# Attention times v in four 32-column tiles of the TensorE array instead of two 64-column tiles

## The chip, the cores and the metric

The kernel runs on one core of a Trainium2 chip. Its time is device microseconds (us) of one launch, as the median of several runs; the profile is one further execution, taken by the hardware profiler. PE is TensorE (matrix products and transposes), PEld its weight loads, DVE is VectorE, ACT is ScalarE, POOL is GpSimd, SP is SyncE, which issues most DMAs. L509 is line 509 of the kernel before; the change adds one line, so everything from L509 on has a number larger by one in the kernel after (L509 is L510 there, L519 is L520).

## The reference

The input is `q`, `k`, `v` of shape (4, 8, 768, 64): four batches, eight heads, 768 tokens, 64 numbers per head, all fp32. Two stages are computed.

```python
# attention: the first n_global = 8 keys, and the last n_local = 96 up to the query
scores = q @ k.T / sqrt(64) - slope[h] * dist          # masked outside the window
a      = softmax(scores)
x      = (a @ v)                                       # to (3072 tokens, 512)
# router and experts: one of 8 experts per token, by cosine similarity
logits = xn @ en.T / tau;  e = argmax(logits);  gate = softmax(logits)[e]
out    = gate * (relu(x @ w1[e]) @ w2[e])              # w1 512 x 1024, w2 1024 x 512
```

## The kernel before

**Two stages in time.** The window attention (`window_attention`) fills the time up to about 174 us of the profiled execution; the experts, at 512 to 576 slots each, take the rest. The change lies in the attention.

**How the attention is tiled.** A *group* is one batch with four heads (a half `m` of the eight); there are eight groups. The four heads are two *pairs* `a`, each with two heads `e`. A *unit* is a block `j` of 96 keys, eight per group, together with 30 copied rows of the global keys, which makes 126 rows (`ROWS`). A key block is seen by its own 96 queries and the next 96, so a unit has 192 columns of queries (the last one 96). A *step* works on two units of a group; there are 32 steps, and the order of work on PE, ACT, DVE and SP is written out by hand and kept (`manual_schedule` with these four engines). POOL is not among them in the attention: a planner places POOL's instructions, by times that it assumes for the others.

**What a step does.** `score` (L480) multiplies keys and queries into PSUM, in tiles of 64 rows by 32 columns of the array; `grow` (L486, ACT) takes the exponential into the tile `ex`; `weigh` (L493, DVE) multiplies it by a table of biases. Transposes on PE (L455, L550, L568, L582; full 128x128 array) turn k, q and the results of earlier groups. `attend` then works on the two units of the step before:

- products with v (L509): for each unit part and each pair `a`, one matmul for each of the two heads `e`. The weights are 126 rows by 64 columns of `v`, the moving operand is 192 or 96 columns of `ex`, and the output is 64 partitions of the PSUM tile `od[a]`;
- in every second step, the sums of the denominators (L519) for the parts of two steps: four matmuls per part, whose weights are 126 rows by 32 columns of the constant `halves`, and whose outputs lie side by side in four strips of 32 partitions of `od[2]`.

After the denominators, `od` is copied out (L524, L525, L530, L532). In some steps the experts' scores of an earlier half batch follow on PE (L559), also in weights of 32 columns (`enb`) with 128 rows, in four strips.

Each fp32 matmul appears in the trace as two weight loads and two MATMUL records: 288 matmuls of L509 are 576 records, and so are the 288 of L519.

**What else hangs on the change.** `load_v` loads each group's v by SP two groups ahead; its L430 on POOL copies the 30 global rows into all eight blocks, before the first L509 of that group. POOL also issues the scatters of the router's slots into DRAM (L257), each paced behind a step's score matmuls, and the square root of the router's norms (L224, `pow`), which DVE's L234 waits for.

Of the kernel before, what the change touches and what calls it, by code (L numbers as in the profile page):

```python
# [34 lines left out]
ROWS = BLK + GLB  # L35
# [341 lines left out]
def window_attention(k, ctx):  # L377
# [3 lines left out]
    nc, tc, NT, D, B, S, H, E = k.nc, k.tc, k.NT, k.D, k.B, k.S, k.H, k.E  # L381
# [113 lines left out]
    def attend(g, p, split=True):  # L495


        if p % 2 == 0:
            g.od = [po_p.tile([P, 512], F32, name="od%d" % i, tag="od%d" % i) for i in range(3)]
            k.free = g.od[2][:, QB * BLK :]  # L500
        parts = []
        if p == 2:
            parts.append((g.units[3], 0, BLK, 2 * BLK, True))
        for j in (2 * p, 2 * p + 1):
            parts.append((g.units[j], (j % QB) * BLK, 0, BLK if j % QB == QB - 1 else 2 * BLK, j == 0))
        for u, at, c0, c1, first in parts:
            for a in range(2):
                for e in range(2):
                    nc.tensor.matmul(g.od[a][e * D : (e + 1) * D, at : at + c1 - c0],  # L509
                                     lhsT=g.v[0:ROWS, 2 * a + e, u.j, :],  # L510
                                     rhs=u.ex[:, e, a, c0:c1], start=first, stop=True,
                                     skip_group_check=True)

        g.parts = parts = (g.parts if p % 2 else []) + parts
        for u, at, c0, c1, first in parts if p % 2 else []:
            for a in range(2):
                for e in range(2):
                    i = 2 * a + e
                    nc.tensor.matmul(g.od[2][32 * i : 32 * i + 32, at : at + c1 - c0], lhsT=k.halves[0:ROWS, g.m].rearrange("p i c -> p (i c)"),  # L519
                                     rhs=u.ex[:, e, a, c0:c1], start=first, stop=True,  # L520
                                     skip_group_check=True)
        if p % 2:
            xd = xd_p.tile([P, 2, QB * BLK], F32, name="xd", tag="xd")
            nc.scalar.copy(out=xd[:, 1, :], in_=g.od[1][:, 0 : QB * BLK])  # L524
            (nc.vector.tensor_copy if split else nc.scalar.copy)(out=xd[:, 0, :], in_=g.od[0][:, 0 : QB * BLK])  # L525
            g.xd.append(xd)
            h, den = p // 2, g.batch.den
            if g.m == 0:
                den[h] = den_p.tile([P, QB * BLK], F32, name="den", tag="den")
                nc.vector.tensor_copy(out=den[h][:], in_=g.od[2][:, 0 : QB * BLK])  # L530
            else:
                nc.vector.tensor_tensor(out=den[h][:], in0=g.od[2][:, 0 : QB * BLK], in1=den[h][:], op=ALU.add)  # L532
# [146 lines left out]
    for g in groups:  # L679
        g.units = []  # L680
        for j in range(NB):
            u = Net()
# [54 lines left out]
    for g in groups:  # L737
        gi = groups.index(g)
        pieces = [(g, a, i) for a in range(2) for i in (0, 2, 3, 1)]
        at = [4 * gi - 4 + i // 2 for i in range(8)]  # L740
        if gi == 0:
            pieces, at = [(g, a, i) for i in (3, 1) for a in range(2)], [0, 0, 1, 1]
        elif gi == 1:
            at = [2, 2, 2, 2, 3, 3, 3, 3]
        elif gi == 2:
            at = [5, 5, 5, 6, 6, 6, 7, 7]
        elif gi == len(groups) - 1:
            pieces = [(g, a, i) for i in (0, 2, 3, 1) for a in range(2)]
            at = [4 * gi - 4 + i for i in (0, 0, 0, 0, 1, 1, 2, 2)]
# [5 lines left out]
    for s, (g, p) in enumerate(steps):  # L755
# [60 lines left out]
        if s > 0:  # L816
            q, qp = steps[s - 1]
            attend(q, qp, s < len(steps) - 10)
            if q.m == 1 and qp % 2:
                waiting.append((prev, qp // 2))  # L820
# [15 lines left out]
    for hf in active:  # L836
        half_turns(hf)
        half_router(hf)
    attend(*steps[-1])
    scatter_later(k, len(k.later))  # L840
    hf = start_half(t, 1)
# [915 lines left out]
```

## Time and profile before

| | us |
|---|---|
| median of 3 runs (lowest, highest) | 528.84 (524.05, 530.36) |
| the profiled execution, its own time | 523.84 |
| its span, first to last instruction | 522.0 |
| busy PE / PEld / DVE / ACT / POOL | 498.9 / 411.8 / 301.8 / 197.5 / 152.5 |
| products with v, L509: PE busy, 576 records | 46.6 |
| sums of denominators, L519: PE busy, 576 records | 23.5 |

The first three rows are times of whole launches; the span leaves out 1.84 us around the instructions. Busy time of PE counts the time in which at least one matmul was under way, with its latency, so records that run side by side in different tiles of the array are counted once. The mean granted TensorE clock of the profiled execution is 0.997 of full speed.

### The profile page before, as it was taken

To read this page: it belongs to the slowest core of one execution; us is meant where nothing else is said; L and a number is where in the kernel's file an instruction comes from. 1 tells how busy PE (TensorE), PEld (TensorE's weight loads), DVE (VectorE), ACT (ScalarE), POOL (GpSimd) and SP (SyncE) were. 2 spreads that over 40 slices of the span, in tenths; PEclk is the share of its full clock that TensorE was granted. 3 is DMA by queue.
4 is the path that set the end of the run, shared out by engine and by line. 5 is a ranking of instruction groups with operands and counts; after the bars stand their busy time and mean duration, and the time that the engine had idled before them with its cause. 6 is when DMAs were issued, how large, how long until landed. Compare 5 with 4: busy or idle time off the path is not lost.

```text
span 522.0 us, 13699 instructions
## 1 busy us (share of the span) xinstructions
PE 498.9 (96%) x5606; PEld 411.8 (79%) x5606; DVE 301.8 (58%) x601; ACT 197.5 (38%) x494; POOL 152.5 (29%) x169
## 2 busy tenths in 40 slices
PE   8999999999988998999989999999999999999994
PEld 7777887876766687878878669989899689859963
DVE  5646777766786664938735616756656555615531
ACT  4966766767654321403212212322323222311210
POOL 4211121151364436353430034054043040022031
PEclk9999999999999999999999999999999999999998
DMA  9989988988632536767291028267075073001002
GB/s 171 198 186 174 225 227 209 219 189 201 153 103 79 151 58 151 240 209 265 85 331 44 2 68 317 106 211 249 4 240 218 4 247 139 2 25 58 0 22 68
DMA packets 111421, 76.32 MB, mean 146 GB/s; under 512 B 87077, under 2 KB 95269, under 8 KB 111281
## 3 DMA queue, kind: packets, MB, share of 16 engines
q1 hardware_dynamic: 102769, 59.00, 42.8%
q0 software_dynamic: 6912, 15.26, 9.0%
q8 instruction: 63, 1.03, 0.9%
q14 instruction: 77, 0.63, 0.5%
q10 hardware_dynamic: 1600, 0.39, 0.3%
HBM read 61.66 MB, written 17.16 MB: 151 GB/s over the span
## 4 chain that ended last, share of the span: by engine, by line
PE 56%; issue 2%; DVE 1%; DMA 1%; POOLq 0%; POOL 0%; DVEq 0%
PE big L1295 24%; PE big L1102 12%; PE work L1228 7%; PE work L1102 5%; PE work L1241 4%; PE work L1012 2%; PE big L1271 2%; DMA xg<-x_dram,idss 1%; PE work L1022 1%; POOL xg L986 0%; POOLq L1722 0%; DVE wsum L1041 0%; DVE y L1113 0%; DVE xsum L1042 0%; DVE xT L1041 0%
## 5 line engine op out<-in xcount | busy, mean ns | idle before, releaser
L493 DVE TENSOR_TENSOR ex<-ex,table 126x768 f32<-126x768 f32 x64 | 60.7, 955 | 41.8 <-ACT ex L486 41.2
L1307 DVE TENSOR_TENSOR hT<-big,hT 128x320 f32<-128x320 f32 (+4 forms) x70 | 39.3, 565 | 43.5 <-PE big L1295 42.1
L1247 POOL DMA_INDIRECT out_dram<-y_arm,tids x17 | 17.0, 1001 | 161.4 <-ACT y_arm L1230 120.1
L1295 PE MATMUL big<-xT,w1t 128*128 128x160 f32 (+4 forms) x336 | 59.4, 330 | 2.2 <-issue 2.2
L486 ACT ACTIVATE ex<-pa 126x384 f32<-126x384 f32 (+1 forms) x128 | 53.5, 476 | 21.1 <-PE pa L480 15.1
L1295 PEld LDWEIGHTS big<-xT,w1t 128*128 128x128 f32 x336 | 54.2, 190 | 4.9 <-issue 3.1
L986 POOL DMA_INDIRECT xg<-x_dram,idss x32 | 36.6, 1143 | 49.3 <-PE work L1012 15.9
L509 PE MATMUL od<-ex,v 126*64 126x192 f32 (+1 forms) x576 | 46.6, 305 | 0.2 <-issue 0.2
L480 PE MATMUL pa<-qT,kT 64*32 64x128 f32 (+3 forms) x2048 | 39.9, 268 | 2.5 <-issue 2.5
L480 PEld LDWEIGHTS pa<-qT,kT 64*32 64x32 f32 (+1 forms) x2048 | 30.1, 106 | 14.5 <-issue 10.9
L509 PEld LDWEIGHTS od<-ex,v 126*64 126x64 f32 x576 | 34.8, 136 | 8.2 <-issue 4.5
L1295 PE MATMUL big<-xsum,fsum 128*128 128x160 f32 (+4 forms) x224 | 39.7, 330 | 1.2 <-DVE hT L1307 1.2
L1015 ACT COPY xT<-work 128x256 f32<-128x256 f32 x56 | 18.0, 376 | 57.5 <-PE work L1012 54.0
L257 POOL DMA_INDIRECT meta<-mt,slot x24 | 27.7, 1153 | 39.7 <-DVE rd L553 20.0
L1295 PEld LDWEIGHTS big<-xsum,fsum 128*128 128x128 f32 x224 | 36.1, 190 | 2.6 <-DVE hT L1307 1.4
L1228 PE MATMUL work<-w2t,hT 128*128 128x512 f32 x80 | 35.1, 593 | 0.0
L430 POOL COPY v<-v 30x896 f32<-30x896 f32 (+1 forms) x15 | 16.5, 1111 | 53.2 <-DMA v<-in_v_dram 29.8
L1102 PE MATMUL big<-wsum,hsum 128*128 128x256 f32 x136 | 31.1, 380 | 0.7 <-ACT ptmp L1127 0.5
L1309 ACT ACTIVATE hT<-hT 128x320 f32<-128x320 f32 (+4 forms) x42 | 21.7, 533 | 25.1 <-DVE hT L1307 24.9
L1102 PEld LDWEIGHTS big<-wsum,hsum 128*128 128x128 f32 x136 | 25.7, 190 | 5.3 <-issue 1.0
L1228 PEld LDWEIGHTS work<-w2t,hT 128*128 128x128 f32 x80 | 15.1, 190 | 17.7 <-issue 17.6
L1106 DVE TENSOR_TENSOR ptmp<-big,ptmp 128x256 f32<-128x256 f32 x16 | 6.8, 422 | 37.6 <-ACT ptmp L1127 17.0
(245 smaller groups left out, 901.2 us busy)
## 6 DMA issues: line engine op xcount, KB each, us to landing
w1t<-in_moe_w_dram SPq DMA_DIRECT2D x6, 2048.0 KB
w2t<-in_moe_w_dram SPq DMA_DIRECT2D x6, 2048.0 KB
v<-in_v_dram SPq DMA_DIRECT2D x32, 192.0 KB
x_dram<-xs SPq DMA_DIRECT2D x23, 256.0 KB
k<-in_k_dram SPq DMA_DIRECT2D x28, 192.0 KB
q<-in_q_dram SPq DMA_DIRECT2D x28, 192.0 KB
w1t<-in_moe_w_dram SPq DMA_DIRECT2D x32, 128.0 KB
w2t<-in_moe_w_dram SPq DMA_DIRECT2D x32, 128.0 KB
```

The lines of the kernel that those rows point to most:

```text
L257: i = nc.gpsimd.indirect_dma_start(out=k.meta[:], out_offset=bass.IndirectOffsetOnAxis(ap=slot[:, t : t + 1], axis=0), in_=mt[:, t, :], in ...
L480: i = nc.tensor.matmul(u.sp[e][k0:k1, a * n + c0 : a * n + c1], lhsT=t.kT[rows, j, k0:k1], rhs=t.qT[rows, j * BLK + c0 : j * BLK + c1], st ...
L486: nc.scalar.activation(u.ex[:, e], u.sp[e][0:ROWS, 0 : 2 * u.n].rearrange("p (a c) -> p a c", a=2), AF.Exp, scale=k.scale)
L493: nc.vector.tensor_tensor(out=exv, in0=exv, in1=tab[:, :, 0 : u.n // BLK, :], op=ALU.mult)
L509: nc.tensor.matmul(g.od[a][e * D : (e + 1) * D, at : at + c1 - c0], lhsT=g.v[0:ROWS, 2 * a + e, u.j, :], rhs=u.ex[:, e, a, c0:c1], start=f ...
L986: i = k.nc.gpsimd.indirect_dma_start(out=xg[:], out_offset=None, in_=k.x_dram[0 : upto or k.N + 1, :], in_offset=bass.IndirectOffsetOnAxis ...
L1102: self.k.nc.tensor.matmul(ps, lhsT=x[:, f, :], rhs=w[:, f, :], start=f == 0 and not add, stop=True, skip_group_check=True)
L1228: nc.tensor.matmul(ps[:], lhsT=hT[:, f, j * P : (j + 1) * P], rhs=w2[:, f, :], start=i == 0, stop=i == k.NF - 1)
L1241: nc.tensor.matmul(ps[i * size : (i + 1) * size, 0:m], lhsT=hT[:, f, base : base + size], rhs=w2[:, f, i * m : (i + 1) * m], start=o == 0, ...
L1295: nc.tensor.matmul(to[f // 2][:, f % 2 * 256 : f % 2 * 256 + h], lhsT=x[:, l, f * P : (f + 1) * P], rhs=y[:, l, 0:h], start=not (add or f ...
L1307: nc.vector.tensor_tensor(out=to, in0=x, in1=z, op=ALU.add)
L1309: nc.scalar.activation(to, to, AF.Relu)
```

## The change

Each product with v (126 rows, 64 weight columns) is cut into two of 32 weight columns. The four products of a pair `a` then go to the four 32-partition strips of `od[a]`, in the order of the strips, as L519 does with `od[2]`. Inputs, outputs, the moving operands and the number of columns that stream are as before; 288 matmuls become 576.

```diff
         for u, at, c0, c1, first in parts:
             for a in range(2):
-                for e in range(2):
-                    nc.tensor.matmul(g.od[a][e * D : (e + 1) * D, at : at + c1 - c0],
-                                     lhsT=g.v[0:ROWS, 2 * a + e, u.j, :],
+                for i in range(4):
+                    e, d = i // 2, i % 2 * 32
+                    nc.tensor.matmul(g.od[a][32 * i : 32 * i + 32, at : at + c1 - c0],
+                                     lhsT=g.v[0:ROWS, 2 * a + e, u.j, d : d + 32],
                                      rhs=u.ex[:, e, a, c0:c1], start=first, stop=True,
                                      skip_group_check=True)
```

The order of instructions on PE (apart from L509 itself), DVE, ACT and SP is the same in the two built programs. On POOL the planner's order differs in the attention. With s for a scatter (L257), v for a copy of global rows (L430) and P for the `pow` (L224), the stretch from the first scatter on reads

```
before  s s v s v s s s P v v s s s v s s v P s s s P s s s s
after   s s v v s s s s v P v s s v s v s s P s s s P s s s s
```

Four copies stand one or two scatters earlier, and the first P in it stands behind a copy that it was ahead of. One copy of an early group also comes ahead of the two small copies of L161.

## The prediction

> **What bounds the kernel now.** I read the engines' busy row first, then the busy time by stage, then which waits end PE's idle time, and only then the changed lines.
>
> ```profile
> PE 498.9 (96%) x5606; PEld 411.8 (79%) x5606; DVE 301.8 (58%) x601; ACT 197.5 (38%) x494; POOL 152.5 (29%) x169
> ```
>
> ```profile
> core 0: us, PE busy (x) PEld busy (x) DVE busy (x) ACT busy (x) POOL busy (x), PEclk, DMA share, GB/s
> 16.00:60.00 44.00, 42.70 (x1015) 33.88 (x1018) 27.02 (x42) 32.90 (x86) 7.96 (x11) 1.00 0.99 192
> 60.00:100.00 40.00, 39.50 (x949) 31.67 (x942) 29.03 (x63) 27.39 (x74) 8.71 (x7) 1.00 0.92 222
> 100.00:140.00 40.00, 38.66 (x873) 30.16 (x873) 26.84 (x67) 26.29 (x70) 13.62 (x13) 1.00 0.88 195
> 140.00:174.00 34.00, 30.44 (x683) 22.87 (x664) 23.89 (x75) 17.11 (x48) 15.13 (x14) 1.00 0.38 110
> ```
>
> The second view has a row per stretch of the attention: its length, each engine's busy time, the granted clock, the DMA share. PE idles 1.3, 0.5, 1.3 and 3.6 us, 6.7 of 158, so PE sets the attention's pace; the 3.6 us at its end are mostly waits for ACT's and DVE's results. The DMA engines are full to 130 us, but PE's waits name no DMA there: v for the group that starts at 114 us was issued by 87 us. So what PE loses or gains in L509 counts nearly whole, up to the last third.
>
> **What a product costs.** Busy time can't tell, since tiles overlap. I take the matmuls in order of time (start, length, line, records):
>
> ```profile
> 20.52 1.20 PE L509 MATMUL od<-ex,v 126*64 126x192 f32 x16
> 21.65 1.35 PE L519 MATMUL od<-ex,halves 126*32 126x192 f32 x32
> 22.93 1.13 PE L480 MATMUL pa<-qT,kT 64*32 64x128 f32 x64
> ...
> 59.57 1.35 PE L519 MATMUL od<-ex,halves 126*32 126x192 f32 x32
> 60.73 0.83 PE L559 MATMUL pa<-xd,enb 128*32 128x384 f32 x8
> ...
> 83.22 1.85 PE L509 MATMUL od<-ex,v 126*64 126x96 f32 x24
> 85.00 0.85 PE L559 MATMUL pa<-xd,enb 128*32 128x384 f32 x8
> ```
>
> ```profile
> L509 PE MATMUL od<-ex,v x576: 246/326/378, 16.3 to 171.8; 126*64 126x192 f32 x128, 126*64 126x96 f32 x64
> ...
> L519 PE MATMUL od<-ex,halves x576: 246/326/350, 21.7 to 173.2; 126*32 126x192 f32 x127, 126*32 126x96 f32 x65
> ```
>
> The last view gives min/median/max of a record: 246 ns with 96 columns and 326 with 192, the same in both tilings.
>
> A *slot* is the time from one set of side-by-side records to the next. The L509 block of 16 records (20.52 to 21.65) has four pairs of 192 columns and four of 96; the block of 24 (83.22 to 85.00) has eight and four. Their difference, 1.78 - 1.13 = 0.65 us over four pairs, makes a slot of 192 columns 162.5 ns; with 80 ns less for 96 (326 - 246) it is 82.5. The single records' starts agree: pairs start 6 to 8 ns apart, then 155 ns pass.
>
> The L519 block of 32 (21.65 to 22.93) would in pairs hold 12 x 162.5 + 4 x 82.5 = 2.28 us; it takes 1.28. In fours it holds 6 x 162.5 + 2 x 82.5 = 1.14, and 0.14 is left for its ends. So **four tiles of 32 columns take the slot of two of 64**.
>
> The ends are the second reading. Block L509 of 16: 4 x 162.5 + 4 x 82.5 = 0.98, so 0.15 of its 1.13 us are ends. About 50 ns of it lies at the entry: the longest first record is 378 where the median is 326. In 32-column tiles the entry is 24 ns (350 against 326), as the weights to be loaded are half as wide. [...] A change of lines inside one tiling has no exit: L519 to L559 (59.57 to 60.73) takes 1.16 us where L519 to L480 takes 1.28.
>
> **The change part by part.**
>
> *Streaming.* L509 has 384 records of 192 columns and 192 of 96: 192 and 96 slots, 39.1 us. After it there are 768 and 384, in fours again 192 and 96 slots: 39.1 us. Zero.
>
> *Entries.* L509 begins 31 times in another tiling (32 calls of `attend`, the last two adjoining): 31 x (50 - 24) = 0.8 us less.
>
> *Exits that vanish.* 16 times L519 follows L509, 5 times L559 does, both in 32 columns and all rows. Each such border loses the 100 ns exit and the 24 ns entry: 21 x 124 = 2.6 us less.
>
> *Exits that stay.* Ten times L480 follows. The last of four records starts 20 ns after the first instead of 7: 10 x 13 ns = 0.1 us more.
>
> Sum on PE: -0.8 - 2.6 + 0.1 = **-3.3 us**.
>
> *More instructions.* 576 more weight loads and 576 more matmul records. The row for their issue is L519, and L480 with 64 records in 1.13 us: 18 ns a record. [...] L519's fours take 82.5 ns, 21 ns a record, and start 7 ns apart: I take the row, zero. [...]
>
> *What doesn't reach the end.* PE's idle gaps close on other engines' results; when PE comes earlier it may wait longer. Between all (-3.3) and none (0) I take all up to 140 us, and none of the last quarter, about 7 of 31 blocks: 0.7 us lost, -2.6. The rest of the program follows the last `attend` through the router, its scatters and the gathers, so it shifts along.
>
> *POOL's order.* Copies of v stand earlier among the scatters, and each copy waits until the scatters ahead of it have landed: at 104.53 a copy ran 7.0 us after a scatter's issue, here 5.7 us after the second one's (138.16):
>
> ```profile
> 143.88 0.93 POOL L430 COPY v<-v 30x896 f32<-30x896 f32 x1 [4.39 <-issue]
> 144.90 0.88 POOL L224 TENSOR_TENSOR ss<-ss,half 128x3 f32<-128x3 f32 x1
> 145.98 1.09 POOL L257 DMA_INDIRECT meta<-mt,slot  x1 [0.20 <-issue]
> ```
>
> ```profile
> 146.53 0.16 DVE L234 TENSOR_SCALAR ss<-ss 128x3 f32<-128x3 f32 x1
> ```
>
> The L224 at 144.90 feeds the L234 at 146.53, with 0.75 us to spare. In the new order a scatter at 129.26, a copy 5.7 to 7.0 us later, a scatter, another copy 5.7 to 7.0 later, and two scatters of 1.3 us come before this L224: it ends between 146.4 and 149.2. DVE, which keeps the written order, is held 0 to 2.7 us there; behind L234 stand the rest of the router and the next L493, whose `ex` PE wants a step later. I take 1.2 held, half of it reaching PE: +0.6. The L224 at 111.41 now stands behind the copy of 116.16 and ends by 118.5; its L234 is at 120.60: nothing. The copies themselves come earlier, so no L509 waits for them.
>
> Sum: -3.3 + 0.7 + 0.6 = **-2.0 us**, 521.8 for the profiled execution's 523.84 (its span of 522.0 and 1.84 around it, which nothing here touches). That execution is 5.0 below the median of the runs (528.84; 524.05 to 530.36); on the median the forecast is **526.8 us**. No change of less than about 2% (10.6 us) can be told from none in this kernel.
>
> **The rivals.**
>
> *Lost in other waits.* PE comes 3.3 us earlier, and ACT, DVE and the loads don't. For: DVE and ACT are busy 65 to 75% to 140 us, with a chain score, exponential, weighing, product in each step. Against: PE idles 3 us in 124 there. Time 528.8.
>
> *POOL's order takes it back: slower than before.* If the second copy waits 7.0 us for a scatter issued at 138.2, L224 ends near 148.7, the next one (153.25, for an L234 at 154.67) slips as well, and DVE is held 2 to 4 us in a stretch in which PE already waits for it. From 2.6 us passed on to PE the kernel is slower; at 4, +1.4: 530.2. Against: one step's results are made ahead, which hides part.
>
> [...]
>
> *The edit gives more*, by steps that begin earlier throughout the attention: -3.3 whole and up to 3 us of PE's gaps as well, -6: 522.8.
>
> **How the numbers follow.** Forecast (-4 to -1): 0.55. Lost in other waits (-1 to +0.5): 0.18. POOL (up to +3): 0.14. Fours fail: 0.06. More: 0.07, of which 0.03 over 2%. The range, 520.5 to 531.5, runs from -6 (with the 2 us by which the runs' medians differ) to the POOL case, and leaves out the fours. Chances: faster by over 2% 0.03, within 0.90, slower 0.07.
>
> **What would show it.** Right: L510 with 1152 records, blocks 26 ns shorter at their entry, and an L510 block with the L520 or L560 block behind it 150 ns shorter together; the longest record near 350 ns, not 378; the end of the last L520 about 2 us earlier; no wait of DVE for L224 over 2 us. Wrong: records of L510 that start in pairs, the same block lengths at the borders to L520, or a wait of PE in the attention that wasn't there.

## The result

| | before | after |
|---|---|---|
| median of 22 runs each, on one chip, us (lowest, highest) | 528.76 (524.05, 531.5) | 527.32 (523.89, 531.08) |
| the profiled execution, its own time, us | 523.84 | 529.14 |
| its span, us | 522.0 | 527.4 |
| mean granted clock | 0.997 | 0.994 |

The ratio after to before is 0.9987, 95% interval 0.9964 to 1.0009: no change that can be told from none (-1.9 to +0.5 us). The forecast was 526.8 us. The two profiled executions mislead at first sight: that of before lies 4.9 us under its median, that of after 1.8 over its own, so they differ by 5.3 us in the wrong direction. What an interval of times can't resolve, the trace must show.

The engines' busy row and the stages of the attention, after:

```profile
PE 500.3 (95%) x6182; PEld 410.1 (78%) x6182; DVE 301.4 (57%) x601; ACT 197.6 (37%) x494; POOL 152.5 (29%) x169
```

```profile
core 0: us, PE busy (x) PEld busy (x) DVE busy (x) ACT busy (x) POOL busy (x), PEclk, DMA share, GB/s
16.00:60.00 44.00, 42.95 (x1272) 33.98 (x1273) 27.67 (x44) 33.35 (x88) 8.15 (x11) 1.00 0.94 190
60.00:100.00 40.00, 37.81 (x1004) 29.54 (x995) 28.18 (x61) 26.04 (x70) 10.96 (x9) 1.00 0.93 210
100.00:140.00 40.00, 37.91 (x971) 29.60 (x971) 26.42 (x67) 26.52 (x71) 10.25 (x9) 1.00 0.88 207
140.00:174.00 34.00, 29.09 (x718) 20.95 (x711) 20.46 (x63) 15.91 (x42) 15.90 (x15) 0.95 0.42 93
```

There are 576 more records and as many more loads. PE idles 1.1, 2.2, 2.1 and 4.9 us in the four stretches, 10.2 where it was 6.7, and in the last one the granted clock is 0.95.

**The blocks.** The matmuls in order of time (start, length, line, records):

```profile
20.90 1.19 PE L510 MATMUL od<-ex,v 126*32 126x192 f32 x32
21.91 1.32 PE L520 MATMUL od<-ex,halves 126*32 126x192 f32 x32
23.16 1.13 PE L480 MATMUL pa<-qT,kT 64*32 64x128 f32 x64
...
42.54 1.84 PE L510 MATMUL od<-ex,v 126*32 126x96 f32 x48
44.20 0.83 PE L560 MATMUL pa<-xd,enb 128*32 128x384 f32 x8
```

From the start of the L510 block to the L520 block is 1.01 us where it was 1.13 (20.52 to 21.65); L520 to L480 is 1.25 where it was 1.28; L510 to L560 is 1.66 where it was 1.78 (83.22 to 85.00). Taken to the nanosecond over all undisturbed blocks, the border L510 to L520 or L560 is 127 shorter, the entry of L520 24.5 shorter, and a block L510 with L480 behind it 13 shorter: the prediction's terms.

**What came instead.** The waits of PE in the attention (16 to 182 us; us in total, times, longest), after and then before:

```profile
PE pa L480 <- issue: 5.4, 12, 1.2
PE pa L455 <- ACT ex L486: 1.4, 3, 0.7
PE pa L551 <- ACT ex L486: 1.3, 1, 1.3
```

```profile
PE pa L480 <- issue: 2.5, 7, 0.9
PE pa L550 <- ACT ex L486: 1.4, 1, 1.4
PE pa L455 <- ACT ex L486: 0.8, 2, 0.5
```

The waits on ACT, DVE and loads sum to 4.5 us after and 5.0 before, by all rows of both views (the first three of each are shown); up to the last denominators alone they are 3.9 and 3.7. So no new wait stands there. What has grown is "issue" ahead of L480, 2.5 to 5.4: PE had nothing to wait for and yet nothing to do. Two of the places in after, in order of time, and the one of this kind in before:

```profile
89.33 1.07 PE L480 MATMUL pa<-qT,kT 64*32 64x128 f32 x55
91.61 0.41 PE L480 MATMUL pa<-qT,kT 64*32 64x128 f32 x9 [1.21 <-issue]
...
111.23 0.85 PE L480 MATMUL pa<-qT,kT 64*32 64x128 f32 x38
113.19 0.63 PE L480 MATMUL pa<-qT,kT 64*32 64x128 f32 x26 [1.10 <-issue]
```

```profile
31.98 1.07 PE L480 MATMUL pa<-qT,kT 64*32 64x128 f32 x55
33.90 0.41 PE L480 MATMUL pa<-qT,kT 64*32 64x128 f32 x9 [0.85 <-issue]
34.25 0.55 PE L455 MATMUL pa<-ident,k 128*128 128x128 f32 x3
```

A block of L480 whose 64 records otherwise start within one microsecond stops after 55, or after 38, and goes on more than a microsecond later, in the middle of a loop with no wait in it. Of the 5.4 us, 2.3 are the two stops shown, and of before's 2.5, 0.85. Most of the rest, 2.8 and 1.5 us, is of another kind, gaps of about 0.3 us that come in rows; they are taken up under what stays open.

### The profile page after: what moved, and what is told of

Its sections match the earlier page's. It is cut to its first block, busy times and chain, and to the rows that moved or that the text cites. A ratio compares the mean times of both kernels' runs of the same rounds, so it can differ in the third digit from the quotient of the medians.

```text
span 527.4 us, 14853 instructions
## 1 busy us (share of the span) xinstructions
PE 500.3 (95%) x6182; PEld 410.1 (78%) x6182; DVE 301.4 (57%) x601; ACT 197.6 (37%) x494; POOL 152.5 (29%) x169
## 4 chain that ended last, share of the span: by engine, by line
PE 78%; issue 5%; DVE 4%; SPq 4%; DMA 4%; ACT 2%; POOL 2%; POOLq 0%; ACTq 0%; DVEq 0%
PE big L1296 24%; PE big L1103 12%; PE work L1229 7%; PE od L510 5%; PE work L1103 5%; PE pa L480 4%; PE work L1242 4%; PE pa L455 3%; PE od L520 3%; PE pa L672 2%; PE work L1013 2%; PE big L1272 2%; DMA q<-in_q_dram 2%; SPq L420 1%; PE pa L583 1%
## 5 line engine op out<-in xcount | busy, mean ns | idle before, releaser
L486 ACT ACTIVATE ex<-pa 126x384 f32<-126x384 f32 (+1 forms) x128 | 53.6, 475 | 24.5 <-PE pa L480 20.2
L987 POOL DMA_INDIRECT xg<-x_dram,idss x32 | 35.4, 1108 | 50.0 <-issue 19.6
L480 PE MATMUL pa<-qT,kT 64*32 64x128 f32 (+3 forms) x2048 | 42.9, 264 | 5.7 <-issue 5.4
L510 PE MATMUL od<-ex,v 126*32 126x192 f32 (+1 forms) x1152 | 47.1, 306 | 0.2 <-issue 0.2
L480 PEld LDWEIGHTS pa<-qT,kT 64*32 64x32 f32 (+1 forms) x2048 | 31.0, 105 | 20.1 <-issue 15.9
L257 POOL DMA_INDIRECT meta<-mt,slot x24 | 26.1, 1086 | 51.5 <-DVE rd L554 24.7
L510 PEld LDWEIGHTS od<-ex,v 126*32 126x32 f32 x1152 | 31.8, 111 | 11.0 <-issue 4.9
L430 POOL COPY v<-v 30x896 f32<-30x896 f32 (+1 forms) x15 | 18.2, 1219 | 54.2 <-DMA v<-in_v_dram 42.7
L1103 PE MATMUL big<-wsum,hsum 128*128 128x256 f32 x136 | 31.1, 380 | 1.2 <-issue 0.7
L1103 PEld LDWEIGHTS big<-wsum,hsum 128*128 128x128 f32 x136 | 25.7, 190 | 5.8 <-issue 1.5
```

What stands on the lines that cost most here:

```text
L257: i = nc.gpsimd.indirect_dma_start(out=k.meta[:], out_offset=bass.IndirectOffsetOnAxis(ap=slot[:, t : t + 1], axis=0), in_=mt[:, t, :], in ...
L480: i = nc.tensor.matmul(u.sp[e][k0:k1, a * n + c0 : a * n + c1], lhsT=t.kT[rows, j, k0:k1], rhs=t.qT[rows, j * BLK + c0 : j * BLK + c1], st ...
L486: nc.scalar.activation(u.ex[:, e], u.sp[e][0:ROWS, 0 : 2 * u.n].rearrange("p (a c) -> p a c", a=2), AF.Exp, scale=k.scale)
L510: nc.tensor.matmul(g.od[a][32 * i : 32 * i + 32, at : at + c1 - c0], lhsT=g.v[0:ROWS, 2 * a + e, u.j, d : d + 32], rhs=u.ex[:, e, a, c0:c1 ...
L987: i = k.nc.gpsimd.indirect_dma_start(out=xg[:], out_offset=None, in_=k.x_dram[0 : upto or k.N + 1, :], in_offset=bass.IndirectOffsetOnAxis ...
L1103: self.k.nc.tensor.matmul(ps, lhsT=x[:, f, :], rhs=w[:, f, :], start=f == 0 and not add, stop=True, skip_group_check=True)
```

## Where PE halts: the arrival of its own instructions

The page of the profile has a row for the queue that brings instructions, before and after:

```profile
q8 instruction: 63, 1.03, 0.9%
```

```profile
q8 instruction: 68, 1.11, 1.0%
```

Every packet has 16,384 bytes in both traces (all 63, all 68). The halts shown above, and the others that are counted as halts below, stand at one place in the count of PE's instructions (its loads, its records, and the few of its sequencer, such as semaphores): 192 or 193 more than a multiple of 256 have gone before. I call that place a packet's border: in each profile as many packets come in the attention as borders are crossed, to within one. By that a packet holds 256 of PE's instructions, 64 bytes each, and the 1,152 more (576 records, 576 loads) are 4.5 packets. Packets of q8 and what PE did next, from the trace (us):

```
kernel        packet issued   took   landed   PE goes on   idle   landing to going on
before            31.48       0.96    32.44      33.90     0.85        1.46
after             86.74       3.50    90.25      91.61     1.21        1.36
after            110.60       1.12   111.71     113.19     1.10        1.48
after_again       89.71       2.30    92.02      93.41     1.74        1.39
after_again      107.56       0.97   108.54     110.10     2.01        1.56
```

A packet is asked for 1.3 us after PE has crossed the border before, in the median of twelve profiles (from 1.1 us ahead of it to 4.4 behind), lands 0.9 to 1.3 us later in most cases and up to 3.5, and after a halt PE goes on 1.1 to 1.7 us after it landed, in most cases 1.4 to 1.6. Nowhere in the twelve does PE cross a border sooner than 1.0 us after the landing of a packet. In before, the packet of the halt at 33.90 was asked for 2.5 us after the border at 28.98, took 0.96 and PE went on 1.46 after it had landed, 4.9 us in sum; PE had gone through the 256 instructions at hand in 4.1. Ahead of before's other borders it took 4.4 us or more. In after it took 3.3 us ahead of the border at 31.05 and did not halt there: that packet was asked for 0.35 us after the border before and had landed 1.7 us ahead. I read from this that PE halts where it is through with the instructions at hand sooner than these three times are over. What sets the moment at which a packet is asked for is not shown. In the attention of before, a border is crossed every 5.8 us in the mean (27 packets); after, every 5.1 (32). The mean hides the stretches that count: a block L480 is 128 instructions in 1.06 us, and with the change an L510 block next to it holds twice as many as it did, in the same time (32 records in 1.00 us to the next block where 16 took 1.13). In before PE passes all but one of the borders without a halt; below, in a kernel with more instructions (flood96), it halts at 20 of 37.

**The second cost, the clock.** The clock of after around 166 us (length, PE busy with its records, granted clock, DMA share, GB/s):

```profile
164.00:166.00 2.00, 0.89 (x16) 1.00 0.65 55
166.00:168.00 2.00, 2.00 (x23) 0.59 0.06 16
168.00:170.00 2.00, 2.00 (x41) 0.56 0.25 54
```

After a stretch in which PE was busy 0.89 of 2 us the clock is granted at half for 3.41 us: (1 - 0.59) x 2 + (1 - 0.56) x 2 = 1.7 us lost. In the attention of before there is no such stretch. The gaps ahead of it stand at no packet border, so this loss is not one of arrival. Ahead of it went gaps of 0.3 to 0.45 us in a row, and in another execution (after_again, below) a single one of 2.0. Nor is the halved clock a mark of the change: over the runs, the mean granted clock is 0.9940 in after's 22, and 0.9938 to 0.9943 in before's 11, 17 and 23 beside the experiments (on one chip, 12 runs each, late20_after has 0.9908 and late20_before 0.9928).

## The experiments

Theory: the borders between blocks give back the 3.3 us of the prediction, and the arrival of the 1,152 added instructions takes them away. Rival A: the instructions cost nothing, and the long profile of after was a bad execution. Rival B: the load of the DMA engines up to 130 us makes the packets late, not their number. The experiments ran on other chips than the result, each beside runs of before on the same chip, which took 522.2 to 522.6 us there, 6 less than on the first chip.

**The two kernels again**, one profile each.

> The unchanged kernel once more, for a second profile. Supply theory: PE halts without any semaphore in the middle of an L480 block, at the border of a 16 KB packet of instructions, and goes on 1.3 to 1.5 us after the packet has landed; 0 to 2 such halts of over 0.3 us in the attention, as in the first profile (one, 0.85 us). Rival (halts are waits for ACT or DVE): halts at any place, none tied to a packet.

> The changed kernel once more, for a second profile. Supply theory: 2 to 4 halts of over 0.3 us at packet borders in the attention, 1.5 to 3 us in all, against 0 to 1 us in the kernel before. Rival (halts are waits for ACT or DVE): the two halts of 1.2 and 1.1 us of the first profile don't come back at packet borders.

Measured: 522.49 and 524.29 us, spans 520.7 and 522.6 (the runs of before beside them: median 522.3, 518.83 to 524.74). The profile of after is the longer one again. From the first L509 to the start of the last L519 record before took 151.69 us and after 158.69; halts at borders (of 0.1 us or more) were one of 0.57 us against four of 4.29, three of them over 0.3 us, more than the 1.5 to 3 us expected. The clock was halved twice, from 111.3 (1.2 us behind the end of the halt of 2.01) and from 159.1, at the end of a wait of 1.91 us for ACT. Only the first stands behind a halt; and before_again has the same wait for ACT of 1.91 us with no halved clock behind it.

**Only every second step in four tiles** (`odd`, and once more on another chip as `odd_again`). Of the 21 borders between L510 and a block in its tiling 16 are gained, 2.4 us by the block lengths, with 512 instructions added, two packets.

```diff
-                for i in range(4):
-                    e, d = i // 2, i % 2 * 32
-                    nc.tensor.matmul(g.od[a][32 * i : 32 * i + 32, at : at + c1 - c0],
-                                     lhsT=g.v[0:ROWS, 2 * a + e, u.j, d : d + 32],
+                w = 32 if p % 2 else D
+                for i in range(2 * D // w):
+                    e, d = i * w // D, i * w % D
+                    nc.tensor.matmul(g.od[a][w * i : w * i + w, at : at + c1 - c0],
+                                     lhsT=g.v[0:ROWS, 2 * a + e, u.j, d : d + w],
```

> Tiles of 32 columns only in the steps whose denominators follow (16 of 32), two tiles of 64 in the others. Half of the added instructions, and 16 of the 21 borders: 16 x 124 ns and 15 entries x 26 ns, -2.4 us on PE. Supply theory: about half of the halts that the whole change adds, so 1 to 2 us faster than before. Rival (the gain is lost in waits for ACT and DVE whatever the instructions): 0 to 0.7 us faster, as the whole change.

Measured: ratio 0.9998 (0.9954 to 1.0042).

> The kernel odd once more, since six runs with one at 526.63 left its time open. Supply theory: 1 to 2 us faster than before (medians), with 0 to 2 halts at packet borders. Rival: no difference.

Measured: ratio 1.0024 (1.0002 to 1.0046). The expectation of a gain missed. The attention took 152.54 and 151.13 us, with halts of 2.07 and 1.38 us: what these steps gain is gone as well. Why it doesn't come out ahead of the whole change, with fewer halts, is seen behind the attention (below).

**More instructions, no other change of the work.** Two kernels cut the same products into more pieces by columns, one from before (`split48`: 64-column tiles, 48 moving columns each) and one from after (`flood96`: every 192 columns in two of 96).

```diff
 # split48, in the kernel before
-                for e in range(2):
-                    nc.tensor.matmul(g.od[a][e * D : (e + 1) * D, at : at + c1 - c0],
+                for x in range(c0, c1, 48):
+                    for e in range(2):
+                        nc.tensor.matmul(g.od[a][e * D : (e + 1) * D, at + x - c0 : at + x - c0 + 48],
...
 # flood96, in the kernel after
-                for i in range(4):
+                for x in range(c0, c1, BLK):
+                    for i in range(4):
...
+                        nc.tensor.matmul(g.od[a][32 * i : 32 * i + 32, at + x - c0 : at + x - c0 + BLK],
```

> The kernel before with each product with v cut along its columns into pieces of 48, still in two tiles of 64: 2688 more instructions in the attention, 2.3 times what the change adds, and no border changes. By the slots it costs 192 x 7.5 + 96 x 2.5 ns = +1.7 us if instructions are free. Supply theory: +5 to +12 us, with halts at most packet borders in the attention. Rival (instructions are free): +1 to +2.5 us and no more halts at packet borders than before.

Measured: 545.94 us, ratio 1.048 (1.0435 to 1.0526), some 25 us more, well over the expectation. The experiment is confounded: its slots are longer than its columns.

```profile
59.42 2.07 PE L510 MATMUL od<-ex,v 126*64 126x48 f32 x64
61.42 1.13 PE L480 MATMUL pa<-qT,kT 64*32 64x128 f32 x64
...
64.05 1.61 PE L510 MATMUL od<-ex,v 126*64 126x48 f32 x48
65.58 0.70 PE L520 MATMUL od<-ex,halves 126*32 126x192 f32 x12
```

32 pairs in 2.00 us and 24 in 1.53 make a slot of 0.47 / 8 = 58 ns, where a scaling of 82.5 and 162.5 by columns gives some 42. Over 960 slots that is 15 us which have nothing to do with packets (what sets the 58 ns is not shown). The rest, about 10 us, stands beside nine halts of 7.72 us and two halved clocks. This run alone proves little.

> The changed kernel with its products with v also cut along the columns, 192 into two of 96, in the same fours of 32 weight columns: 1536 instructions more than the changed kernel, 2688 more than the kernel before. By the slots (82.5 ns for 96 columns, over the 58 ns that split48 showed as the floor for 64 weight columns) it costs 192 x 2.5 ns = +0.5 us on the changed kernel. Supply theory: +5 to +12 us on the kernel before, with 8 or more halts at packet borders. Rival (instructions are free, split48 was slow by its weight loads alone): -2 to +1 us on the kernel before.

Measured: 536.22 us, ratio 1.0259 (1.0216 to 1.0302), 13.5 us over before, somewhat more than expected. Streaming can't be it: two slots of 96 columns against one of 192 are 2 x 82.5 - 162.5 = 2.5 ns, 192 times, 0.5 us. The trace agrees: an undisturbed block with v ahead of the denominators takes 1.014 us here and 1.004 in after_again. The row of instructions and PE's waits in the attention (16 to 190 us):

```profile
q8 instruction: 74, 1.21, 1.0%
```

```profile
PE pa L480 <- issue: 9.0, 10, 2.1
PE od L511 <- issue: 5.7, 5, 2.1
PE od L217 <- issue: 1.8, 1, 1.8
PE od L521 <- issue: 1.2, 2, 0.8
```

All borders between blocks are as in after, the records are those of after cut in two, and the 1,536 added instructions, six packets, bring 20 halts of 18.45 us in sum where after has 2.3 to 4.3. The halts are no longer in L480 alone: they come wherever the border falls. Rival A falls: instructions are not free.

**Fewer instructions.** The scores of the global keys are left out of both kernels (their weights in the table of biases are zero; the exponential, the weighing and the products with v work on all 126 rows as before). With such sums the kernel takes its slow way afterwards, a dense attention: its whole time, 6.87 ms for both, says nothing here, and only the first 170 us of the profiles are read.

```diff
-        bands.append((BLK, ROWS, 0, BLK))
...
-    nc.vector.tensor_scalar_mul(loc[G, 0:3, :], loc[G, 0:3, :], gm[G])
+    nc.vector.memset(loc[G, 0:3, :], 0.0)
```

> The kernel before without the scores of the global keys (the fourth band of L480, whose tiles run beside the other three; their weights in the table are zero, so the global keys are left out of the attention): 1024 instructions less in the attention, nearly no PE time less. The router then sees other values, so the time of the experts may change, in the same way as in noglob_after. Supply theory: no halts at packet borders of over 0.3 us. Rival: the 0.6 to 0.85 us halt near 34 us stays.

> The changed kernel without the scores of the global keys, as noglob_before: 1024 instructions less, which leaves it with 128 more than the kernel before. Supply theory: 0 to 1 halts at packet borders, so the border gain arrives: 2.3 to 3.3 us faster than noglob_before, in the end of the attention and in the time. Rival (gain lost in waits for ACT and DVE): 0 to 1 us faster than noglob_before.

Measured: the attention takes 151.40 us in two-tile form, with no halt at all, as expected, and 152.31 us in four-tile form, with three halts of 1.56 us, where 0 to 1 halts and a gain of 2.3 to 3.3 us were expected. The 28 packets of the latter are about as many as before's 27, which has halts of 0.57 and 0.85: the expectation that the halts go with the number of packets missed. That the density of the instructions just ahead of a border counts beside it fits, but no run tried it alone. Nor do the halts explain this pair: the gain of 3.3 us less 1.6 would leave the four-tile form shorter, and it is 0.9 longer, though it also had no halved clock and the other one had one. Its waits for ACT, DVE and loads are some 0.9 us longer; the rest has no name.

**The DMA engines relieved** (rival B). The loads of the experts' weights are moved out of the attention's steps, to its last one (`late31`) or to step 20 and behind (`late20`), in both kernels.

```diff
-                if s >= 11 and weights:
+                if s >= 31 and weights:      # late31; in late20: s >= 20
...
-        weights_part()                       # late20, at both places
+        weights_part(2)
```

> The kernel before with no loads of expert weights during the attention (they follow from its last step on, so the time as a whole is longer by 10 to 30 us and only the attention is read). Supply theory with the DMA engines' load as the reason why packets are late: no halt at a packet border after 70 us, where the weights are loaded otherwise. Rival (packets are late by the density of the instructions alone): as in before_again, one halt near 34 us, which this edit doesn't touch.

> The changed kernel with no loads of expert weights during the attention. DMA load as the reason: the halts between 70 and 130 us (2.3 and 4.1 us in the two profiles of the changed kernel) are gone, and the attention from the first L509 to the last L519 is 2.5 to 3.3 us shorter than in late31_before. Rival (density alone): 1 to 4 us of halts at packet borders stay.

Measured: 535.33 and 536.54 us, both some 13 us longer than before, as the experts' weights come late. The attention takes 151.49 and 152.32 us, with halts of 0.19 and 1.71 us.

> The kernel before with the loads of expert weights begun in step 20 instead of 11, two pieces at each place instead of one, so that 48 instead of 42 pieces are issued in the attention, where the DMA share is 0.4 instead of 0.9. If DMA load makes the packets late: 0 to 1 us faster, since this kernel has few halts. Rival (density alone): no difference.

> The changed kernel with the same later loads of weights. If DMA load makes the packets late: 2 to 4 us faster than the kernel before, since the border gain of 3.3 us then arrives. Rival (density alone): as the changed kernel, 0 to 1 us faster.

Measured: ratios 1.0003 (0.9979 to 1.0028) and 1.0016 (0.998 to 1.0051); attention 151.58 and 156.75 us, halts 1.26 and 6.89. In this execution of late20_after no packet between 70 and 135 us took over 1.35 us, and it has ten halts, the most of any kernel with after's instructions. A packet need not be slow for PE to halt: behind one of 1.12 us it halted for 1.10 (after, 110.60), behind one of 0.97 for 2.01 (after_again, 107.56), and behind the one of 3.50 for 1.21. The relief was only partial, though: between 70 and 135 us the mean busy share of the DMA engines is 0.90 in before and 0.91 in after, 0.84 and 0.85 in the late20 pair, and 0.71 and 0.70 in the late31 pair, and late31_after has the least halts, in us, of the four profiles with after's instructions on PE. So slow packets are not the main reason; that the load of the DMA engines has a part in it is not excluded. No version here beats both kernels.

**All of it side by side.** Halts are PE's idle times of 0.1 us or more at packet borders. Each row is one profile. The attention's length runs from the first L509 to the start of the last L519 record.

| kernel | packets in the attention | halts, us | halved clock | length, us |
|---|---|---|---|---|
| before | 27 | 1, 0.85 | 0 | 156.90 |
| before_again | 27 | 1, 0.57 | 0 | 151.69 |
| late20_before | 27 | 3, 1.26 | 0 | 151.58 |
| late31_before | 27 | 1, 0.19 | 0 | 151.49 |
| odd / odd_again | 29 | 4, 2.07 / 2, 1.38 | 0 | 152.54 / 151.13 |
| after | 32 | 2, 2.31 | 1 | 162.50 |
| after_again | 32 | 4, 4.29 | 2 | 158.69 |
| late20_after | 32 | 10, 6.89 | 0 | 156.75 |
| late31_after | 32 | 4, 1.71 | 0 | 152.32 |
| flood96 | 37 | 20, 18.45 | 0 | 171.48 |

In all four pairs the four-tile kernel halts longer: 2.31, 4.29, 6.89, 1.71 us against 0.85, 0.57, 1.26, 0.19, in the mean 3.80 against 0.72; without the global keys it is 1.56 against none. Those 3.1 us of idle are nearly the 3.3 us of the gain. A halt costs 0.2 to 0.4 us more than its idle, too: the block of L480 with before's halt of 0.85 us takes 2.27 us (31.98 to 34.25), an undisturbed one 1.06. If the blocks in which a border falls are held against the shortest that the profiles show of the same block, the borders cost 5.4, 8.1 and 2.8 us more in after_again, late20_after and late31_after than in their partners: the gain of 3.3 us is gone or nearly gone in each, and the attention is longer in all four pairs.

**Given back behind the attention.** In two pairs the span differs by much less than the attention's end: 1.9 us for 6.5 (after_again), 2.8 for 5.0 (late20_after). One reason stands in the waits of PE from 200 us on, of before (the view of before_again has the same line) and of `odd`:

```profile
PE big L1295 <- issue: 2.2, 1, 2.2
```

```profile
PE big L1297 <- issue: 2.4, 1, 2.4
```

Here too PE waits for a packet: in before it was issued at 264.56, took 1.12, and PE went on at 267.39, 1.71 us after it landed. It is the first product of an expert's code, of which the kernel picks one by width at run time. The wait is in before, before_again, late20_before (2.3) and in odd (in odd_again 1.0 is left), and in none of after, after_again, late20_after, flood96 and split48; the late31 pair agrees, with 2.2 us in late31_before and none in late31_after. The alignment would explain this: 512 added instructions are two whole packets and leave the later borders where they were; 1,152 are four and a half, and 2,688 (flood96, split48) ten and a half, which moves every later border by half a packet. So some 2.2 us of the change's standing would be luck of where a border falls, and odd doesn't have them. In before_again the clock is halved from 265.6 on, 1.3 us behind this wait. No kernel was run that shifts the borders by half a packet and does nothing else: that the alignment does it is read from these twelve profiles, not tried.

## Why the prediction was right, and where not

The number was right, 526.8 for 527.32 us and the class "no change". The way to it was right in its gains and wrong in what takes them back. That the sum came out so near is in part luck: the term put at nothing cost about as much as the borders gain or more (5.4, 8.1 and 2.8 us in three pairs), and a wait of 2.2 us behind the attention, which nobody had counted, went away.

- **Streaming, zero: right.** Undisturbed blocks have the lengths that slots of 162.5 and 82.5 ns give, with four tiles in a slot. With that "fours fail" (0.06) fell.
- **Entries and exits, -3.3 us: right, within a few nanoseconds a border, in undisturbed blocks.** 127 ns measured for 26 + 124 less the 24 of the entry that shows a block later; 13 for 26 - 13 where L480 follows. No run shows what fills the 100 ns of the exit, which is what the entry leaves of a block's 0.15 us of ends; the runs show the border as a whole, 1.131 us from an L509 block of 16 to L519 in before and 1.004 in after. The longest record of L510 up to 100 us:

```profile
L510 PE MATMUL od<-ex,v x640: 246/326/351, 16.1 to 99.1; 126*32 126x192 f32 x108, 126*32 126x96 f32 x52
```

  351 ns for the 350 of the prediction, 378 before. The weight loads themselves take 110 ns in the median in 32 columns and 137 in 64, which fits the 26 ns of the entry.
- **More instructions, zero: this step failed.** I took the cost from L519's and L480's rows (21 and 18 ns a record), and as far as they go rightly: the added records make no undisturbed block longer (1.004 us to the L520 block where it was 1.131). But those rows show how fast PE issues what it already has. I did not ask how fast instructions arrive. The term should have been some +3 us of idle in the attention, plus 0.2 to 0.4 us for each halt. Before's own profile had the hint: 63 packets in q8, and a halt of 0.85 us at 33.90 in the middle of a block of L480, under "issue" in the waits. I also read the 3.6 us of idle at the attention's end as mostly waits for ACT and DVE; 1.5 of them are "issue" ahead of L480.
- **POOL's order, +0.6: did not come.** DVE's wait for the square root is the same, 1.5 us once, in both profiles:

```profile
DVE ss L234 <- POOL ss L224: 1.5, 1, 1.5
```

  The L224 that was to be late ran from 145.86 to 146.75, inside the 146.4 to 149.2 that I gave for its end, and held nobody. The rival that rests on it fell.
- **Idle gaps, +0.7, and the rival "lost in other waits":** the time fits that rival too (528.8 lies in the interval), but its mechanism isn't there: up to the last denominators, waits on ACT, DVE and loads are 3.9 us for 3.7.
- **"The rest of the program shifts along": not so.** It became shorter by 0.6 us (from the last L519's start to the end of PE's last matmul, 341.5 to 340.9) between the first two profiles, and by 5.0 (344.8 to 339.8) between the second two. In after of the first pair, new "issue" waits, one of 0.7 us at L1103 and two of 0.3 at L1242, fill most of the place of the one at L1295. Of the 5.0, 2.2 are the lost wait at L1295, 1.7 by estimate the halved clock behind it, and 0.8 a shorter wait for DVE's xd.
- **The end of the last L520, "about 2 us earlier": wrong.** It started its last record at 178.56 in place of 173.24.

**What stays open.** How often PE halts in an average run: a kernel has one or two profiles here, and halts of kernels with the same instructions on PE vary from 1.7 to 6.9 us. Why a packet takes 1 us in one place and 3.5 in another. And the blocks of L480 that break up into gaps of 0.3 us at no packet border, as at 144.9 and 162.4 us in after and at 159.0 in before: rows of such gaps are only in the two profiles of the first chip (single ones of 0.4 us are in odd and late31_after too), cost 2.6 to 2.9 us each, and are in after once more often than in before, which is half of the 5.6 us by which those two attentions differ. In sum the terms for the second pair, by block lengths, are -3.3 (borders between tilings), +4.5 (blocks with halts), +0.7 (two shorter stops at packet borders, near 31.5 and 131.2 us), and +3.2 (blocks under the two halved clocks, of which one stands behind a halt): 5.1 of the 7.0 us by which its attentions differ. The other 1.9 are spread over transposes and scores away from packet borders, most of them before 72 us, and have no name.

## What to carry to other kernels

When a change adds instructions to an engine, cost their arrival as well as their issue: count the instructions between two packet borders in the densest stretch and hold the time PE takes for them against a packet's way (here about 1.3 us until it is asked for, 0.9 to 1.3 until it lands, and 1.4 to 1.6 more until PE goes on, some 4 us in sum). Cutting a product into tiles to join its neighbour's tiling was worth just the time that went between two tilings, here 0.127 us a border, so it pays only where that is more than the added instructions cost. Look for "issue" in the waits in the middle of a block that has no wait: here that is the place that more instructions made worse (ahead of L480 2.5 us in before, 5.4 in after, 9.0 in flood96).

## What the runs showed of the hardware that was not expected

- PE's instructions come in packets of 16,384 bytes, and after a halt PE goes on 1.1 to 1.7 us after the landing of the one that it needs. With 27 packets in 151 to 157 us it halts one to three times; with 32, two to ten times; with 37 in 171 us (flood96), 20 times.
- A halt of 2.2 to 2.4 us (1.0 in odd_again) some 90 us behind the changed stretch is there in the six profiles whose added instructions are whole packets or none, and in none of the six in which they shift the borders by half a packet.
- The clock was granted at half for 3.41 us after a run of gaps of 0.3 to 0.45 us (after), and for some 3.4 us after a single halt of 2.0 us (after_again, from the granted 0.83, 0.50 and 0.82 of three stretches of 2 us). It did not always follow: flood96 has halts of 2.07 and 2.09 us and no halved clock in its attention.
- Pairs of 64-column weights with 48 moving columns took 58 ns a slot in split48, where 42 was the estimate from the slots of 82.5 and 162.5 ns.
